# Gathering the attention matmuls of a tile step on TensorE ahead of 18 expert matmuls, from tile 16 on

## The chip, the cores and the metric

One core of one Trainium2 chip. The metric is the device time of one execution, in microseconds; lower is better.

## The reference, cut to what matters

Batched attention (8 batches, 8 heads, 512 local and 32 global tokens, head size 64) feeds an expert layer on its 8 x 544 output rows.

```python
s_g = scale * np.matmul(q_g, k_all.transpose(0, 1, 3, 2))       # global queries see all 544 keys
out_g = np.matmul(sm(s_g), v_all)
mask = np.abs(pos[:, None] - pos[None, :]) <= 32                # local queries: a band, and the 32 global keys
s_l = np.concatenate([s_lg, np.where(mask, s_ll, -1e9)], axis=-1)
out_l = np.matmul(sm(s_l), np.concatenate([v_g, v_l], axis=2))
h = np.maximum(np.maximum(x @ w1, x @ w2), x @ w3)              # x: 4608 rows of the attention's output, 512 wide; 768 wide inside
return h @ w_out
```

## The kernel before

A **tile** `sl` is 128 local queries of a pair `p` of heads; there are 128 tiles, four to a pair (`t = sl % 4`), sixteen to a batch `b`. The main loop (L506 to L535) makes one **step** per tile, and in a step TensorE serves several tiles at different stages, plus the expert layer of the batch before:

- **T**: `trans(sl + 1)` (L334), four 128x128 transposes of the next tile's probabilities, which a DMA put into `prob`. They go to the PSUM tile `T`, which ScalarE copies to `pt` (high part, L102) and from which VectorE subtracts (low part, L94).
- **S**: `scores(sl + 3)` (L300), four matmuls (two in the first tiles) into a PSUM tile `S`; VectorE reduces them (L322), ScalarE takes the exponential (L324), VectorE the reciprocal (L326, L327), GpSimd scales (L112), and a DMA stores to `prob` (L330).
- **O**: `pv(sl)` (L373), four value products of this tile with `pt` and `vs`, into `O`.
- **g**: `glob(p + 1, t)` (L262), in steps with `t` of 0 and 1 alone: two matmuls with the global queries of the next pair, of 384 columns at `t = 0` and 160 at `t = 1`, into a PSUM tile `S` as well. At `t = 2`, `glob_soft` (L285) finishes their softmax and stores it with six small DMAs to `probg`.
- **G**: `transg(sl + 1)` (L356), one 128x128 transpose of a third of `probg` into a PSUM tile `S`. ScalarE copies the wanted part to the last 32 columns of `pt` (L102), VectorE subtracts (L94).
- **L**: `fill(n)` (L470) takes `n` matmuls of the expert layer (L421: 216 per batch, then L440: 72), each 128x128 times 128x512. 18 per step make a batch's 288 in 16 steps.

Splitting into a high and a low part is how full fp32 accuracy is kept; the first 26 to 28 tiles skip it in part (`NATK`, `NAT`). From step 16 on the scores run three tiles ahead; before (`EARLY`) they run further ahead.

Tiles come from pools, and a pool with `bufs=n` hands out n buffers in turn: a new tile waits until every reader of the tile that last had its buffer is done. **`S` has two buffers (L61), shared by S, g and G**; `T` and `O` have one each, `pm` (the expert layer's sums) three. All eight PSUM banks are taken.

Every engine takes its instructions in a fixed order, which a scheduler sets when the kernel is built, mostly that of the code; where it reckons that an instruction isn't ready it lets later ones pass. `copy`, `sub` and `times` (L89 to L112) pick the engine by a running tally of each engine's load. All DMAs are issued by SyncE (SP) in one queue.

The kernel ends with the last batch's expert layer and that of the global rows (L537), without attention work beside them.

Of the kernel before, what the change touches and what calls it, by code (L numbers as in the profile page):

```python
# [47 lines left out]
def f32(ap):  # L48
    return ap.bitcast(F32)


def body(ctx, tc, kin, qin, vin, min_, w1, w2, w3, w4, out):
# [31 lines left out]
    def settle(ns):  # L84
        top = max(load.values()) - ns
        for e in load:
            load[e] = max(load[e], top)

    def sub(out, a, b, psum=False):  # L89
        n = width(out)  # L90
        c = {"d": n * 1.04 + (160 if psum else 110)}
        if not psum:
            c["p"] = n * 2.32 + 130
        (dve if least(c) == "d" else pool).tensor_tensor(out=out, in0=a, in1=b, op=ALU.subtract)  # L94

    def copy(out, a, psum=False):
        n = width(out)
        c = {"d": n * (1.04 if psum else 0.52) + (160 if psum else 150), "a": n * 0.833 + (150 if psum else 190)}
        if least(c) == "d":
            dve.tensor_copy(out=out, in_=a)  # L100
        else:
            act.copy(out=out, in_=a)  # L102
# [107 lines left out]
    EARLY, AHEAD = 16, 9  # L210
    kraw, kst, qraw, qs, vraw, vs, xr, sc, pg, pts = [{} for _ in range(10)]

    def load_k(p):
        if p < B * NP:
            if 4 * p in NATK:
                kraw[p] = att.tile([128, KW + 2 * SG], F32, name="kn", tag="kst")
            else:
                kraw[p] = att.tile([128, KW + 2 * SG], F32, name="kraw", bufs=1)
            nc.sync.dma_start(out=kraw[p], in_=kin[p])

    def split_k(p):
        if p >= B * NP or 4 * p in NATK:
            return
        r = kraw.pop(p)
        g = r[:, KW:].rearrange("p (j g) -> p j g", j=2)
        t = qgz
        copy(t[:, :, 0:SG], g)
        sub(t[:, :, 64:64 + SG], g, f32(t)[:, :, 0:SG])
        t = kst[p] = att.tile([128, 2, KW], F32R, name="kst")
        copy(t[0:64, 0], r[0:64, 0:KW])  # L230
        copy(t[64:128, 1], r[64:128, 0:KW])
        sub(t[64:128, 0], r[0:64, 0:KW], f32(t)[0:64, 0])
        sub(t[0:64, 1], r[64:128, 0:KW], f32(t)[64:128, 1])
# [21 lines left out]
    def split_v(s):  # L255
        if NAT <= s < NS:
            v = vraw.pop(s)
            t = vs[s] = att.tile([128, 4, 2, D], F32R, name="vs")
            copy(t[:, :, 0], v)
            sub(t[:, :, 1], v, f32(t)[:, :, 0])  # L260
# [24 lines left out]
    def glob_soft(p):  # L285
        if p >= B * NP:
            return
        s, nm, z = pg[p]
        dve.tensor_tensor(out=nm[:, 0:1], in0=nm[:, 0:1], in1=nm[:, 1:2], op=ALU.min)
        act.activation(out=s, in_=s, func=AF.Exp, bias=nm[:, 0:1], scale=-1.0, accum_out=z[:, 0:1])  # L290
        dve.tensor_scalar(out=z[:, 0:1], in0=z[:, 0:1], scalar1=1e-9, scalar2=None, op0=ALU.add)
        dve.reciprocal(out=z[:, 0:1], in_=z[:, 0:1])
        spend("d", 220)
        spend("a", 760)
        times(s, s, z[:, 0:1])

        for c0, n, i, h, d0 in GPUT:
            nc.sync.dma_start(out=f32(probg[p % 2])[64 * h:64 * h + 64, i, d0:d0 + n], in_=s[:, c0:c0 + n])
# [35 lines left out]
    def trans(sl):  # L334
        if sl >= NS:
            return
        s = sc.pop(sl)
        ps = psT.tile([128, 512], F32, name="T")
        pr = ps.bitcast(F32R)
        for j in range(2):  # L340
            for c in range(2):
                i = pe.transpose(pr[:, 256 * j + 128 * c:256 * j + 128 * c + 128], s[:, j, 128 * c:128 * c + 128], identr)  # L342
        if sl == EARLY:

            ctx.enter_context(tc.issue_after(i.ins))
        src = ps.rearrange("p (x q) -> p x q", q=128)
        if sl < NAT:
            pt = pts[sl] = att.tile([128, 2, 2, 160], F32, name="pt", tag="pt")
            copy(pt.rearrange("p j c q -> p (j c) q")[:, :, 0:128], src, True)
        else:  # L350
            pt = pts[sl] = att.tile([128, 2, 2, 2, 160], F32R, name="pt", tag="pt")
            v = pt.rearrange("p j c a q -> p (j c) a q")
            copy(v[:, :, 0, 0:128], src, True)
            sub(v[:, :, 1, 0:128], src, f32(v)[:, :, 0, 0:128], True)

    def transg(sl):  # L356
        if sl >= NS:
            return
        p, t = divmod(sl, 4)
        pt = pts[sl]  # L360
        i, h, n = GCH[t]
        g = psS.tile([128, 512], F32, name="S")
        pe.transpose(g.bitcast(F32R)[:, 0:128], probg[p % 2][:, i], identr)  # L363
        src = g[:, 64 * h:64 * h + 64 * n].rearrange("p (c j g) -> p c j g", j=2, g=SG)
        if sl < NAT:
            copy(pt.rearrange("p j c q -> p c j q")[:, 0:n, :, 128:160], src, True)
            return
        v = pt.rearrange("p j c a q -> p c j a q")
        hi, lo = v[:, 0:n, :, 0, 128:160], v[:, 0:n, :, 1, 128:160]
        copy(hi, src, True)  # L370
        sub(lo, src, f32(hi), True)
# [39 lines left out]
    def moe_group(xs, n, stores):  # L411
        hh = []
        for f in range(6):
            ht = moe.tile([128, 2, 512], F32R, name=f"h{f}", tag=f"h{f}")
            m = moe.tile([128, 512], F32, name="m", tag="m")
            for i in range(3):
                ps = pm.tile([128, 512], F32, name="pm")
                q = 0
                for k in range(4):
                    for w, a in ((wh, 0), (wh, 1), (wl, 0)):  # L420
                        pe.matmul(ps[:, 0:n], lhsT=w[f][:, i, k], rhs=xs[k][:, a, 0:n], start=(q == 0), stop=(q == 11))  # L421
                        q += 1
                        if q < 12:
                            yield
                if i == 0:
                    copy(m[:, 0:n], ps[:, 0:n], True)
                else:
                    spend("d", n * 1.04 + 67)
                    dve.tensor_tensor(out=m[:, 0:n], in0=ps[:, 0:n], in1=m[:, 0:n], op=ALU.max)  # L429
                if i == 2:  # L430
                    copy(ht[:, 0, 0:n], m[:, 0:n])
                    sub(ht[:, 1, 0:n], m[:, 0:n], f32(ht)[:, 0, 0:n])
                yield
            hh.append(ht)
        for t in range(n // 128):
            ps = pm.tile([128, 512], F32, name="pm")
            q = 0
            for f in range(6):
                for a, w in ((0, wo[0]), (1, wo[0]), (0, wo[1])):
                    pe.matmul(ps, lhsT=hh[f][:, a, 128 * t:128 * t + 128], rhs=w[:, f], start=(q == 0), stop=(q == 17))  # L440
                    q += 1
                    if q < 18:
                        yield
            o = moe.tile([128, 512], F32, name="o", tag="o", bufs=2)
            copy(o, ps, True)
            stores(t, o)
            yield
# [3 lines left out]
    def moe_local(b):  # L451
        def st(t, o):
            r = b * TOK + SG + t * 128
            nc.sync.dma_start(out=out[r:r + 128], in_=o)
        return moe_group(xs.pop(b), SL, st)
# [14 lines left out]
    def fill(n):  # L470
        if mm[0]:
            for _ in range(n):
                next(mm[0], None)
# [3 lines left out]
    def next_scores(last):  # L477
        while ahead[0] <= last:
            scores(ahead[0])
            split_q(ahead[0] + 1)  # L480
            load_q(ahead[0] + 4)
            ahead[0] += 1
# [23 lines left out]
    for sl in range(NS):  # L506
        p, t = divmod(sl, 4)
        b, n = divmod(p, NP)
        settle(4500)
        if sl % 16 == 0 and b:  # L510
            fill(400)
            mm[0] = moe_local(b - 1)
        trans(sl + 1)
        fill(4)
        next_scores(max(min(sl + 5, EARLY - 1), sl + 3))
        if t == 2:
            split_k(p + 2)
            load_k(p + 3)
        fill(4)
        pv(sl)  # L520
        if t <= 1:
            glob(p + 1, t)
        elif t == 2:
            glob_soft(p + 1)
        fill(3)
        transg(sl + 1)
        fill(7)
        split_v(sl + 2)
        load_v(sl + 3)
        for _ in range(WS[sl] if sl < len(WS) else 0):  # L530
            weight_step()
        if sl % 16 >= 12:
            i = sl % 16 - 12
            q = b * NP + i
            xs.setdefault(b, []).append(split_x(xr[q][:, :, 0:128], SL))  # L535
# [56 lines left out]
```

## Time and profile before

| | |
|---|---|
| time, median of 3 runs | 860.52 us (859.49 to 860.64) |
| span of the profiled execution | 861.4 us |
| busy: TensorE, VectorE, ScalarE, GpSimd | 94%, 66%, 61%, 59% of the span |
| mean granted TensorE clock | 0.973 of full speed |

The profiled execution's own time is its span, 861.4 us from the first to the last instruction; what lies around it is not in the view, and the span is 0.9 us above the median of the three runs. "PE" is TensorE's matmuls, "PEld" its weight loads, "DVE" VectorE, "ACT" ScalarE, "POOL" GpSimd, "SPq" SyncE's DMA issues. In rows of a timeline stand the start in us from the span's start, the duration, engine, line, operation, output<-inputs, shape and count, and in brackets the engine's idle time before it with what ended it. Matmuls overlap in such rows (a duration holds the way through the array), so TensorE's pace is read from start to start.

### The profile page before, as it was taken

The numbers are of one execution on the slowest core, as the hardware profiler recorded it, in microseconds if no ns is written. First come the engines' busy times: TensorE is split into PE (matmuls) and PEld (weight loads), VectorE is DVE, ScalarE is ACT, GpSimd is POOL, SyncE is SP. The second block draws the span as 40 slices with busy tenths as digits, with TensorE's granted clock in tenths as the row PEclk, the third lists the DMA queues.
The fourth block names the chain that finished last, engine by engine and source line by source line (L and its number), as shares of the span: only waits on it lengthen the run. The fifth ranks groups of instructions, "written<-read, shape, count | busy, mean of one in ns | idle before, by whom it ended". The sixth has DMA issues, their size and how long they took to land.

```text
span 861.4 us, 15721 instructions
## 1 busy us (share of the span) xinstructions
PE 813.0 (94%) x4452; PEld 674.2 (78%) x4452; DVE 566.7 (66%) x1784; ACT 529.1 (61%) x1479; POOL 509.8 (59%) x683
## 2 busy tenths in 40 slices
PE   5866788999999999999999999999999999999997
PEld 3644566778888788888888888888888888888896
DVE  4657699787777677777778677867787676511111
ACT  4656566677767676767776767776776766511111
POOL 4535577786667666776768576766677664411211
PEclk8786999999999999999999999999999999999999
DMA  6586655424333533344333533353334322100000
GB/s 201 166 243 186 190 165 190 146 90 153 103 106 96 160 112 106 100 123 125 104 109 100 150 98 100 96 160 111 112 111 131 121 75 72 62 24 1 25 25 25
DMA packets 107238, 98.53 MB, mean 114 GB/s; under 512 B 21008, under 2 KB 97936, under 8 KB 107152
## 3 DMA queue, kind: packets, MB, share of 16 engines
q1 hardware_dynamic: 107152, 97.53, 37.2%
q8 instruction: 36, 0.59, 0.3%
q14 instruction: 50, 0.41, 0.2%
HBM read 56.85 MB, written 8.91 MB: 76 GB/s over the span
## 4 chain that ended last, share of the span: by engine, by line
PE 82%; DVE 6%; DMA 6%; ACT 2%; issue 2%; SPq 2%; POOL 1%; ACTq 0%; POOLq 0%; DVEq 0%
PE pm L421 45%; PE pm L440 16%; PE O L390 6%; PE S L319 5%; PE T L342 4%; DMA wraw<-w_in 2%; PE S L277 1%; DVE wraw L170 1%; DMA probg<-sg 1%; PE O L383 1%; PE S L363 1%; PE pm L315 1%; DMA early<-s 1%; ACT s L324 1%; PE S L315 1%
## 5 line engine op out<-in xcount | busy, mean ns | idle before, releaser
L421 PE MATMUL pm<-xs,wh 128*128 128x512 f32 (+1 forms) x1296 | 408.0, 388 | 3.3 <-POOL xs L94 3.3
L421 PEld LDWEIGHTS pm<-xs,wh 128*128 128x128 f32 x1296 | 233.6, 189 | 35.3 <-POOL xs L94 3.8
L421 PE MATMUL pm<-xs,wl 128*128 128x512 f32 (+1 forms) x648 | 253.1, 391 | 0.0
L112 POOL TENSOR_SCALAR s<-s,z 128x192 f32<-128x192 f32 (+1 forms) x250 | 113.0, 465 | 98.7 <-ACT lox L102 37.8
L421 PEld LDWEIGHTS pm<-xs,wl 128*128 128x128 f32 x648 | 122.5, 189 | 22.7 <-issue 1.6
L324 ACT ACTIVATE s<-s,nm 128x192 f32<-128x192 f32 (+1 forms) x256 | 118.0, 462 | 26.6 <-DVE nm L322 22.6
L440 PE MATMUL pm<-woh,h 128*128 128x512 f32 x408 | 133.7, 398 | 0.1
L94 POOL TENSOR_TENSOR h<-m,h 128x512 fp32r<-128x512 f32 (+1 forms) x54 | 69.3, 1283 | 95.4 <-ACT h L102 93.9
L429 DVE TENSOR_TENSOR m<-pm,m 128x512 f32<-128x512 f32 (+1 forms) x108 | 71.1, 659 | 72.2 <-PE pm L421 72.0
L94 POOL TENSOR_TENSOR qs<-qraw,qs 128x256 fp32r<-128x256 f32 x100 | 73.8, 749 | 56.3 <-ACT qs L102 45.3
L94 DVE TENSOR_TENSOR pt<-T,pt 128x512 fp32r<-128x512 f32 x102 | 70.5, 691 | 46.4 <-ACT pt L102 44.5
L322 DVE CUSTOM_DVE_ANT_0 s<-S,mask 128x192 f32<-128x192 f32 (+1 forms) x232 | 77.9, 371 | 18.5 <-PE S L315 7.7
L326 DVE TENSOR_SCALAR z<-z 128x2 f32<-128x2 f32 x128 | 52.0, 406 | 49.8 <-ACT s L324 49.2
L440 PEld LDWEIGHTS pm<-woh,h 128*128 128x128 f32 x408 | 74.7, 188 | 12.1 <-POOL h L94 0.5
L440 PE MATMUL pm<-wol,h 128*128 128x512 f32 x204 | 81.8, 401 | 0.0
L94 POOL TENSOR_TENSOR vs<-vraw,vs 128x256 fp32r<-128x256 f32 x102 | 75.8, 744 | 8.2 <-ACT vs L102 4.0
L94 POOL TENSOR_TENSOR kst<-kraw,kst 64x576 fp32r<-64x576 f32 x49 | 70.4, 1436 | 11.8 <-issue 8.2
L102 ACT CAST pt<-T 128x512 fp32r<-128x512 f32 x90 | 52.7, 586 | 36.0 <-PE T L342 36.0
L102 ACT CAST qs<-qraw 128x256 fp32r<-128x256 f32 x100 | 40.5, 407 | 54.8 <-PE S L319 54.3
L390 PEld LDWEIGHTS O<-pt,vs 128*128 128x128 f32 x408 | 66.4, 188 | 9.1
L390 PE MATMUL O<-pt,vs 128*128 128x320 f32 (+1 forms) x408 | 72.8, 300 | 0.0
L342 PEld LDWEIGHTS T<-identr,prob 128*128 128x128 f32 x448 | 50.5, 141 | 25.1 <-DMA prob<-s 2.6
(95 smaller groups left out, 1292.2 us busy)
## 6 DMA issues: line engine op xcount, KB each, us to landing
vraw<-v_in SPq DMA_DIRECT2D x128, 128.0 KB, 2.4
qraw<-q_in SPq DMA_DIRECT2D x100, 128.0 KB, 2.2
prob<-s SPq DMA_DIRECT2D x56, 224.0 KB, 2.4
prob<-s SPq DMA_DIRECT2D x56, 192.0 KB, 2.3
wraw<-w_in SPq DMA_DIRECT2D x18, 512.0 KB, 5.3
out_dram<-o SPq DMA_DIRECT2D x32, 256.0 KB, 2.6
kraw<-k_in SPq DMA_DIRECT2D x25, 320.0 KB, 3.1
qn<-q_in SPq DMA_DIRECT2D x28, 128.0 KB, 3.4
```

What stands on the lines that cost most here:

```text
L94: (dve if least(c) == "d" else pool).tensor_tensor(out=out, in0=a, in1=b, op=ALU.subtract)
L102: act.copy(out=out, in_=a)
L112: pool.tensor_scalar(out=out, in0=a, scalar1=col, scalar2=1.0, op0=ALU.mult, op1=ALU.mult)
L319: pe.matmul(ph[j][:, 0:n], lhsT=qs[sl][:, a, 128 * j:128 * j + 128], rhs=kst[p][:, j, c0:c0 + n], start=(a == 0), stop=(a == 1))
L322: dve.tensor_tensor_reduce(out=s[:, j, 0:n], in0=ph[j][:, 0:n], in1=mask[:, (1, 0, 1, 0)[t], 32 * (t == 0):32 * (t == 0) + n], scale=-0.12 ...
L324: act.activation(out=s[:, j, 0:n], in_=s[:, j, 0:n], func=AF.Exp, bias=nm[:, j:j + 1], scale=-1.0, accum_out=z[:, j:j + 1])
L326: dve.tensor_scalar(out=z, in0=z, scalar1=1e-9, scalar2=None, op0=ALU.add)
L342: i = pe.transpose(pr[:, 256 * j + 128 * c:256 * j + 128 * c + 128], s[:, j, 128 * c:128 * c + 128], identr)
L390: pe.matmul(o[:, j, 0:320].rearrange("p (a q) -> p a q", a=2)[:, :, 0:n], lhsT=vs[sl][:, 2 * j + c].rearrange("p a d -> p (a d)"), rhs=pt[ ...
L421: pe.matmul(ps[:, 0:n], lhsT=w[f][:, i, k], rhs=xs[k][:, a, 0:n], start=(q == 0), stop=(q == 11))
L429: dve.tensor_tensor(out=m[:, 0:n], in0=ps[:, 0:n], in1=m[:, 0:n], op=ALU.max)
L440: pe.matmul(ps, lhsT=hh[f][:, a, 128 * t:128 * t + 128], rhs=w[:, f], start=(q == 0), stop=(q == 17))
```

## The change

From step 16 on (`EARLY`), the transpose G moves from behind the value products up to right behind T, and the 18 expert matmuls, until now in four portions (4 behind T, 4 behind S, 3 behind O and g, 7 behind G), stand in one portion behind everything else. Which instructions are issued does not change, apart from a few copies, subtractions and scalings that the tally gives to another engine.

```diff
+        steady = sl >= EARLY
         trans(sl + 1)
-        fill(4)
+        if steady:
+            transg(sl + 1)
+        else:
+            fill(4)
         next_scores(max(min(sl + 5, EARLY - 1), sl + 3))
...
-        fill(4)
+        if not steady:
+            fill(4)
         pv(sl)
         if t <= 1:
             glob(p + 1, t)
         elif t == 2:
             glob_soft(p + 1)
-        fill(3)
-        transg(sl + 1)
-        fill(7)
+        if steady:
+            fill(18)
+        else:
+            fill(3)
+            transg(sl + 1)
+            fill(7)
```

TensorE in step 68 (`t = 0`, pair 17), from the scores S to the transpose G, before; the PSUM tiles `S` are numbered in the order in which they are made.

```order
L319 MATMUL S_5212<-kst_4742,qs_5153 128x192 x4
L421 MATMUL pm_5207<-xs_4702,wh2_104 128x512
L421 MATMUL pm_5207<-xs_4702,wl2_110 128x512
L421 MATMUL pm_5207<-xs_4796,wh2_104 128x512 x2
L390 MATMUL O_5238<-pt_5129,vs_5119 128x320
L390 MATMUL O_5238<-pt_5129,vs_5119 128x2x128
L390 MATMUL O_5238<-pt_5129,vs_5119 128x320
L390 MATMUL O_5238<-pt_5129,vs_5119 128x2x128
L277 MATMUL S_5252<-kst_5071,qgz_96 128x384 x2
L421 MATMUL pm_5207<-xs_4796,wl2_110 128x512
L421 MATMUL pm_5207<-xs_4871,wh2_104 128x512 x2
L363 MATMUL S_5260<-identr_87,probg1_95 128x128
```

The same step after, from the transposes T to the first expert matmuls:

```order
L342 MATMUL T_5197<-identr_87,prob1_93 128x128 x4
L363 MATMUL S_5205<-identr_87,probg1_95 128x128
L319 MATMUL S_5209<-kst_4741,qs_5153 128x192 x4
L390 MATMUL O_5231<-pt_5129,vs_5119 128x320
L390 MATMUL O_5231<-pt_5129,vs_5119 128x2x128
L390 MATMUL O_5231<-pt_5129,vs_5119 128x320
L390 MATMUL O_5231<-pt_5129,vs_5119 128x2x128
L277 MATMUL S_5245<-kst_5068,qgz_96 128x384 x2
L421 MATMUL pm_5252<-xs_4623,wh2_104 128x512 x2
```

The order in which the step's three `S` tiles are made was S, g, G and is G, S, g. With two buffers, g used to take over the buffer of G of the step before, and now takes over that of G of its own step, with four S and four O between the two and no L; the wait that is built into g's first matmul is for VectorE's reading of that G.

VectorE around T, S and G of this step, before:

```order
L94 TENSOR_TENSOR pt_5202<-T_5197,pt_5202 128x4x128
L322 ISA s_5213,nm_5214<-S_5212,mask_89 128x192
L322 ISA nm_5214 128x1
L322 ISA s_5213,nm_5214<-S_5212,mask_89 128x192
L322 ISA nm_5214 128x1
L326 TENSOR_SCALAR z_5215<-z_5215 128x2
L327 RECIPROCAL z_5215<-z_5215 128x2
L396 TENSOR_TENSOR lox_5244<-O_5238,lox_5244 64x320
L398 TENSOR_TENSOR xr_5239<-O_5238,lox_5244 64x160 x2
L281 ISA sg_5249,nmg_5250<-S_5252,sg_5249 64x384
L281 ISA nmg_5250 64x1
L94 TENSOR_TENSOR pt_5202<-S_5260,pt_5202 128x2x2x32
```

and after:

```order
L94 TENSOR_TENSOR pt_5202<-T_5197,pt_5202 128x4x128
L94 TENSOR_TENSOR pt_5202<-S_5205,pt_5202 128x2x2x32
L322 ISA s_5210,nm_5211<-S_5209,mask_89 128x192
L322 ISA nm_5211 128x1
L322 ISA s_5210,nm_5211<-S_5209,mask_89 128x192
```

The low part of G (`pt<-S`) moved from the end of the step's VectorE work to right behind the low part of T (`pt<-T`), ahead of the reductions of S.

ScalarE, after, in the same step:

```order
L102 CAST pt_5202<-T_5197 128x4x128
L102 CAST h1_5096<-m_5097 128x512
L102 CAST pt_5202<-S_5205 128x2x2x32
L102 CAST kst_5391<-kraw_5073 64x576
L324 ACTIVATE s_5210,z_5212<-s_5210,nm_5211 128x192 x2
L102 COPY lox_5237<-O_5231 64x320
```

The high part of G moved in the same way: it stands behind that of T, in this step with an expert copy (`h`) between them, and ahead of the exponentials; at `t = 1` it stands directly behind that of T.

## The prediction

> **What bounds the kernel now.** I read the page's head first, then the windows by stage, then TensorE's timeline inside one step, and last VectorE's and ScalarE's timelines beside it.
>
> ```profile
> span 861.4 us, 15721 instructions
> PE 813.0 (94%) x4452; PEld 674.2 (78%) x4452; DVE 566.7 (66%) x1784; ACT 529.1 (61%) x1479; POOL 509.8 (59%) x683
> ```
>
> ```profile
> 88.70:191.00 102.30, 89.94 (x477) 68.30 (x478) 81.52 (x209) 66.03 (x177) 72.23 (x77) 0.97 0.50 155
> 191.00:400.00 209.00, 207.89 (x1151) 176.11 (x1151) 154.93 (x505) 149.36 (x421) 143.71 (x201) 1.00 0.40 120
> 400.00:742.00 342.00, 342.00 (x1892) 289.80 (x1891) 256.11 (x834) 241.83 (x683) 233.67 (x326) 1.00 0.36 109
> ```
>
> The columns of the windows are the stretch, its length, the busy time of PE, PEld, DVE, ACT and POOL, the granted clock, the DMA share and GB/s. The changed steps run from about 88.7 us (step 16) to 742 us and fall into two stages. From 191 us on PE is busy for 549.9 of 551 us at full clock: what is put into TensorE's row or taken out of it counts in full, and the other engines have 25 to 30% to spare. Before 191 us weights are still being converted, and PE idles 12.4 of 102.3 us.
>
> PE's pace is read from start to start. Step 68, and at the end O of step 69:
>
> ```profile
> 412.63 0.46 PE L342 MATMUL T<-identr,prob 128*128 128x128 f32 x4
> 412.93 0.70 PE L421 MATMUL pm<-xs,wh 128*128 128x512 f32 x2
> 413.46 0.40 PE L421 MATMUL pm<-xs,wl 128*128 128x512 f32 x1
> ...
> 413.93 0.59 PE L319 MATMUL S<-kst,qs 128*128 128x192 f32 x4
> 414.35 0.41 PE L421 MATMUL pm<-xs,wh 128*128 128x512 f32 x1
> ...
> 415.29 0.69 PE L390 MATMUL O<-pt,vs 128*128 128x320 f32 x4
> 415.82 0.51 PE L277 MATMUL S<-kst,qgz 128*128 128x384 f32 x2
> 416.16 0.40 PE L421 MATMUL pm<-xs,wl 128*128 128x512 f32 x1
> ...
> 416.86 0.22 PE L363 MATMUL S<-identr,probg 128*128 128x128 f32 x1
> 416.91 0.45 PE L421 MATMUL pm<-xs,wl 128*128 128x512 f32 x1
> 417.20 0.63 PE L421 MATMUL pm<-xs,wh 128*128 128x512 f32 x2
> 417.67 0.39 PE L421 MATMUL pm<-xs,wl 128*128 128x512 f32 x1
> ...
> 418.59 0.45 PE L342 MATMUL T<-identr,prob 128*128 128x128 f32 x4
> ...
> 421.26 0.74 PE L390 MATMUL O<-pt,vs 128*128 128x320 f32 x4
> 421.83 0.35 PE L277 MATMUL S<-kst,qgz 128*128 128x160 f32 x2
> ```
>
> Two undisturbed L take 417.67 - 417.20 = 0.47, so one takes 0.235 us. The four T take 0.30 to the next start, and the two L behind them 0.53 where 0.47 is usual: a tail of 0.06. G takes 0.05, and the L behind it 0.29, a tail of 0.055. The four S take 0.42, the four O 0.53 (0.57 in step 69), the two g 0.34 (0.19). There is no gap in the row: L, T, S, O, g and G all stand ready when PE comes to them. The whole step takes 418.59 - 412.63 = 5.96 us.
>
> **The change part by part.**
>
> *What is gained on PE.* The number of matmuls stays. A tail comes where a short matmul is followed by one that must load other weights. T's tail before an L goes; G's stays, since S loads weights of the same size behind it. So a step gains between nothing (T's tail falls on G) and 0.06 us; I take 0.03, as G loads as T does. Over the 98 steps of a full PE row (27 to 124) that is -2.9 us (0 to -5.9). The Trainium skill, "TensorE: Matmul & The Clock Gate", section "LDWEIGHTS (loading the stationary operand)", prices a weight load by its 128 columns alone, 128 / 1.2 GHz = 107 ns, whatever the matmul behind it. The four S, of 192 columns, bear it out at 0.42 / 4 = 0.105 us each, and the four T at 0.30 / 4 = 0.075 do not; by the rule this term would be nothing.
>
> *What is added: g waits for G of its own step.* After the change g takes over the buffer of a G that stands only four S and four O ahead. In PE's row g's turn comes, counted from the start of T, at 0.30 + 0.03 (T) + 0.11 (G with its tail) + 0.42 (S) + 0.53 (O) = 1.39 us at t = 0 and 1.43 at t = 1. But it may start only when VectorE has read G, and the low part of G stands behind the low part of T on VectorE, which needs ScalarE's copy of T. These rows price that chain (ScalarE, then VectorE):
>
> ```profile
> 413.18 0.59 ACT L102 CAST pt<-T 128x512 fp32r<-128x512 f32 x1 [1.39 <-PE T L342]
> 413.67 0.62 ACT L102 CAST h<-m 128x512 fp32r<-128x512 f32 x1
> ...
> 417.96 0.27 ACT L102 CAST pt<-S 128x128 fp32r<-128x128 f32 x1
> ...
> 423.12 0.21 ACT L102 CAST pt<-S 128x64 fp32r<-128x64 f32 x1
> ```
>
> ```profile
> 413.80 0.69 DVE L94 TENSOR_TENSOR pt<-T,pt 128x512 fp32r<-128x512 f32 x1 [0.17 <-ACT pt L102]
> ...
> 418.98 0.28 DVE L94 TENSOR_TENSOR pt<-S,pt 128x128 fp32r<-128x128 f32 x1
> ...
> 423.91 0.23 DVE L94 TENSOR_TENSOR pt<-S,pt 128x64 fp32r<-128x64 f32 x1
> ```
>
> From the start of T (412.63), ScalarE's copy runs from 0.55 to 1.14 and VectorE's subtraction from 1.17 to 1.86; neither waits for more than its input. At t = 0 ScalarE then does `h` (1.04 to 1.66) and the high part of G (1.56 to 1.83), and VectorE the low part from 1.86 to 2.14. At t = 1 there is no `h`: the low part follows at once, 1.79 to 2.02. What a release of PE costs is seen where S waited for ScalarE's reading of a buffer:
>
> ```profile
> 145.16 0.24 ACT L102 COPY pt<-S 128x128 f32<-128x128 f32 x1
> ```
>
> ```profile
> 145.46 1.02 PE L315 MATMUL S<-kn,qn 128*128 128x224 f32 x4 [0.93 <-ACT pt L102]
> ```
>
> 145.46 - 145.40 = 0.06. With that and 0.06 for a weight load that now nothing hides (the tail above), g starts at 2.26 instead of 1.39 at t = 0, 0.87 late, and at 2.14 instead of 1.43 at t = 1, 0.71 late. Behind g on PE stand the step's 18 L, which have everything they need and can't pass it. So a pair loses 1.58 us, and the pairs 8 to 31 (their g runs in steps 28 to 121) are 24: 37.9 us, and 0.7 for step 25, 38.6 in all. Bounds: without the tail, the 0.03 and the `h`, 1.2 a pair, 29 us; with ScalarE or VectorE one operation of 0.6 behind in every other step, 2.2 a pair, 53 us. Nothing else on PE can cover it.
>
> *What the moved copies hold up.* The two `pt<-S` now stand ahead of the exponentials and reductions of S, which costs these at most 0.27 + 0.28 us; but S itself stands four L earlier (0.94 us). The product is needed two steps later. Nothing is lost; without those four L it would be up to 0.5 us a step. Eighteen L in a row finish one or two sums of twelve, of which `pm` holds three, so that VectorE has 24 x 0.235 = 5.6 us to clear one, and PE isn't held there.
>
> *G comes earlier than its data may.* At t = 3, G reads the next pair's `probg`, of which the first and the fourth of six DMAs are needed:
>
> ```profile
> 426.52 3.70 SPq L298 DMA_DIRECT2D probg<-sg  x6
> ```
>
> ```profile
> probg<-sg SPq DMA_DIRECT2D x64, 16.0 KB, 1.8
> ```
>
> ```profile
> 430.07 0.46 PE L342 MATMUL T<-identr,prob 128*128 128x128 f32 x4
> ...
> 434.02 0.22 PE L363 MATMUL S<-identr,probg 128*128 128x128 f32 x1
> ```
>
> The fourth issues at 426.52 + 3 x 0.62 = 428.38 and lands 1.8 later, at 430.2. Now that G comes at 434.02; changed, it would come 0.33 behind T, at 430.40. The chain that leads to these DMAs begins with the g of t = 1, so it lies later by 0.7 at most, as T does, and by up to 0.5 more where it queues behind the moved copies; in the last pair of a batch an output store (L454) also stands between the six on SP, which takes about as long to issue as one of them. It is a tie: 0 to 0.5 us for 24 pairs, 0 to 12; I take 0.1, +2.4, near the landing above.
>
> *The first stage.* Here PE's longest wait is for such a DMA:
>
> ```profile
> 152.40 0.25 PE L363 MATMUL S<-identr,probg 128*128 128x128 f32 x1 [2.71 <-DMA probg<-sg]
> ```
>
> ```profile
> PE T L342 <- DMA prob<-s: 6.5, 5, 2.1
> ```
>
> G now comes 11 L and O earlier, 11 x 0.235 + 0.5 = 3.1 us, for three pairs: up to +9, and some +3 for their g. Against that S stands 0.94 earlier in each step, which can shorten the five waits of T for its DMA by that much each, to -5. I take +3 (-5 to +12), since the quoted wait shows that such a G is awaited.
>
> *Sum.* 861.4 - 2.9 + 38.6 + 2.4 + 3 = 902.5; the median of the runs lies 0.9 below the span, so **901 us**.
>
> **The rivals.** (1) *The wait is covered, and the kernel is faster.* If g's buffer were read within 1.4 us of the start of T, only the lost tails and shorter waits of T would be left: 860.5 - 2.9 - 2 = 856. For it: all the work around is unchanged, and now PE waits for nothing. Against it: T's two readings alone end at 1.86. It decides if VectorE takes G before T, or if g gets another buffer. Chance 0.06.
>
> (2) *The copies or `probg` become the bound.* If ScalarE and VectorE, whose work now comes in one burst behind each cluster, run late into the next T, or G at t = 3 waits its full 0.5, the upper bounds 53, 12 and 12 come together: 33 us above my terms, 934; half of that is 918. DVE's 256.11 of 342.00 us speaks against a lasting queue. Chance 0.08.
>
> (3) *The clock falls.* After the 2.71 us wait above PE was slow:
>
> ```profile
> 153.32 0.63 PE L421 MATMUL pm<-xs,wl 128*128 128x512 f32 x1
> 153.75 0.67 PE L342 MATMUL T<-identr,prob 128*128 128x128 f32 x4
> ```
>
> An L took 0.43 instead of 0.235. If each of the 48 waits of g were followed by some eight such L, 48 x 8 x 0.195 = 75 us would come on top, 976. Against it: after a wait of 1.11 us the clock of its window, 191 to 400 us, stayed at 1.00:
>
> ```profile
> 297.00 0.51 PE L342 MATMUL T<-identr,prob 128*128 128x128 f32 x4 [1.11 <-DMA prob<-s]
> ```
>
> The Trainium skill, same page, section "A second HAM failure mode: psum-queue depth-cycling", says that short idles of PE that recur with every round of a PSUM buffer can throw the clock to half and back, as these would. One wait of 1.11 does not show what 48 do. Chance 0.04.
>
> (4) *No change.* The scheduler keeps the old order, or tails and waits cancel. Its order shows the cluster in every step from 27 on. Chance 0.02.
>
> **How the numbers follow.** My forecast has 0.80. Its own range is 861.4 - 0.9 with 29 to 53 for g and part of the other bounds, 884 to 918; the rivals outside hold 0.2, so this is also the range for 8 in 10. A measurement here tells 0.2%, 1.7 us, from no change. Faster: rival 1, 0.06. Same: 0.02. Slower: 0.92.
>
> **What would show it.** Right: from 191 us on, PE's timeline has an idle of 0.6 to 0.9 us before each g, released by VectorE's `pt` of L94, none in steps with t = 2; step 68 takes about 6.8 us instead of 5.96, and a step without g some 0.03 less than now; VectorE's and ScalarE's busy times stay. Wrong: g follows O within 0.1 us, or PE waits at T or S instead, or the clock falls below 1.00 after 191 us.

## The result and the profile after

| | before | after |
|---|---|---|
| median time, us | 860.0 (857.97 to 860.64, 4 runs) | 903.11 (898.92 to 907.56, 4 runs) |
| span of the profiled execution, us | 861.4 | 902.6 |

The change makes the kernel slower: the ratio of the times is 1.051, with an interval of 1.047 to 1.055. The runs also spread wider, 8.6 us where it was 2.7.

The head of the page of after, to be set against that of before:

```profile
span 902.6 us, 15688 instructions
...
PE 823.6 (91%) x4452; PEld 683.2 (76%) x4452; DVE 542.9 (60%) x1782; ACT 521.0 (58%) x1478; POOL 508.7 (56%) x686
```

No engine got new work: VectorE (by 24 us), ScalarE and GpSimd are busy less than before, and TensorE, with the same 4452 matmuls, is busy 10.6 us more. So the 41.2 us are idle time of PE and matmuls that run slower, and the windows say where. I cut both traces at the T of tile 17 and the T of tile 28, the two ends of the first stage, and at the T of tile 126. First before, then after (columns as in the prediction):

```profile
88.70:173.20 84.50, 72.72 (x384) 54.33 (x385) 65.80 (x162) 52.36 (x138) 56.86 (x59) 0.96 0.56 172
173.20:742.00 568.80, 567.11 (x3135) 479.87 (x3134) 426.76 (x1384) 404.86 (x1144) 392.75 (x544) 1.00 0.37 112
```

```profile
85.00:177.50 92.50, 77.17 (x385) 58.86 (x386) 66.80 (x169) 52.77 (x141) 56.73 (x59) 0.89 0.52 158
177.50:783.50 606.00, 575.86 (x3136) 485.65 (x3135) 402.37 (x1379) 395.84 (x1137) 391.02 (x545) 0.99 0.34 105
```

The first stage costs 8.0 us more and the long second one 37.2. What lies ahead of the first changed step is 3.7 us shorter in this execution, which is no work of the change: the last two experiments below, whose instructions stand in the order of before up to there, took 85.4 us as well, so it was before's profiled execution that started late. The tail behind tile 126 is 0.3 us shorter. In the second stage PE's idle time is read as length less busy time: 568.80 - 567.11 = 1.7 us before, 606.00 - 575.86 = 30.1 us now. PE's waits in that window of after name who it waited for (total us, times, longest):

```profile
PE S L277 <- DVE pt L94: 28.8, 46, 2.6
PE S L363 <- DMA probg<-sg: 1.3, 3, 0.7
```

It is the wait that the prediction had named: g, L277, for VectorE's low part of G, in 46 of the 48 steps that have a g (in steps 48 and 112 g hardly waited: 0.07 us and nothing). One such step, PE's timeline from T to T:

```profile
433.43 0.46 PE L342 MATMUL T<-identr,prob 128*128 128x128 f32 x4
433.72 0.25 PE L363 MATMUL S<-identr,probg 128*128 128x128 f32 x1
433.81 0.66 PE L319 MATMUL S<-kst,qs 128*128 128x192 f32 x4
434.30 0.71 PE L390 MATMUL O<-pt,vs 128*128 128x320 f32 x4
435.63 0.62 PE L277 MATMUL S<-kst,qgz 128*128 128x384 f32 x2 [0.62 <-DVE pt L94]
436.08 0.63 PE L421 MATMUL pm<-xs,wh 128*128 128x512 f32 x2
...
440.22 0.29 PE L342 MATMUL T<-identr,prob 128*128 128x128 f32 x2
```

The same stretch on ScalarE and then on VectorE:

```profile
433.98 0.59 ACT L102 CAST pt<-T 128x512 fp32r<-128x512 f32 x1 [2.05 <-PE S L363]
434.46 0.62 ACT L102 CAST h<-m 128x512 fp32r<-128x512 f32 x1
434.98 0.27 ACT L102 CAST pt<-S 128x128 fp32r<-128x128 f32 x1
```

```profile
434.60 0.69 DVE L94 TENSOR_TENSOR pt<-T,pt 128x512 fp32r<-128x512 f32 x1 [0.28 <-ACT pt L102]
435.28 0.29 DVE L94 TENSOR_TENSOR pt<-S,pt 128x128 fp32r<-128x128 f32 x1
```

The chain is there link by link: T's copy on ScalarE ends at 434.57, `h` follows, G's high part at 434.98, T's low part on VectorE from 434.60 to 435.29, G's low part to 435.57, and g starts 0.06 us later, at 435.63. The bracket shows 0.62 us of idle, less than what the wait costs, since a matmul's row holds its way through the array. From start to start: O began at 434.30 and takes 0.53, so g's turn came at 434.83 and g is 0.80 late. Its two matmuls then take 435.63 to 436.08, 0.45 us where they took 0.34: their first weight load starts with g, at 435.63, where it started 0.12 us ahead of g before (415.70 and 415.82).

### The profile page after: what moved, and what is told of

The parts are those of the page before. It is cut to its first block, busy times and chain, and to the rows that moved or that the text cites. A ratio compares the mean times of both kernels' runs of the same rounds, so it can differ in the third digit from the quotient of the medians.

```text
span 902.6 us, 15688 instructions
## 1 busy us (share of the span) xinstructions
PE 823.6 (91%) x4452; PEld 683.2 (76%) x4452; DVE 542.9 (60%) x1782; ACT 521.0 (58%) x1478; POOL 508.7 (56%) x686
## 4 chain that ended last, share of the span: by engine, by line
PE 71%; DVE 10%; ACT 6%; DMA 5%; issue 3%; POOL 2%; SPq 2%; ACTq 0%; POOLq 0%; DVEq 0%
PE pm L421 40%; PE pm L440 15%; DVE pt L94 4%; ACT pt L102 3%; PE T L342 3%; PE O L390 3%; PE S L277 3%; PE S L319 3%; DMA probg<-sg 2%; PE S L363 1%; PE S L315 1%; DVE wraw L170 1%; PE O L383 1%; PE S L273 1%; DMA wraw<-wo_in 1%
## 5 line engine op out<-in xcount | busy, mean ns | idle before, releaser
L421 PE MATMUL pm<-xs,wh 128*128 128x512 f32 (+1 forms) x1296 | 388.7, 383 | 3.6 <-POOL xs L94 3.6
L421 PEld LDWEIGHTS pm<-xs,wh 128*128 128x128 f32 x1296 | 236.2, 190 | 47.4 <-POOL xs L94 4.1
L421 PE MATMUL pm<-xs,wl 128*128 128x512 f32 (+1 forms) x648 | 247.7, 382 | 0.0
L112 POOL TENSOR_SCALAR s<-s,z 128x224 f32<-128x224 f32 (+1 forms) x253 | 112.5, 458 | 131.3 <-ACT lox L102 75.0
L440 PE MATMUL pm<-woh,h 128*128 128x512 f32 x408 | 128.5, 396 | 0.0
L326 DVE TENSOR_SCALAR z<-z 128x2 f32<-128x2 f32 x128 | 42.1, 329 | 67.3 <-ACT s L324 66.5
L390 PE MATMUL O<-pt,vs 128*128 128x320 f32 (+1 forms) x408 | 74.9, 305 | 0.0
L319 PE MATMUL S<-kst,qs 128*128 128x192 f32 (+1 forms) x400 | 66.5, 288 | 0.0
L398 DVE TENSOR_TENSOR xr<-O,lox 64x160 f32<-64x160 f32 x204 | 64.3, 315 | 2.7
```

What stands on the lines that cost most here:

```text
L112: pool.tensor_scalar(out=out, in0=a, scalar1=col, scalar2=1.0, op0=ALU.mult, op1=ALU.mult)
L319: pe.matmul(ph[j][:, 0:n], lhsT=qs[sl][:, a, 128 * j:128 * j + 128], rhs=kst[p][:, j, c0:c0 + n], start=(a == 0), stop=(a == 1))
L390: pe.matmul(o[:, j, 0:320].rearrange("p (a q) -> p a q", a=2)[:, :, 0:n], lhsT=vs[sl][:, 2 * j + c].rearrange("p a d -> p (a d)"), rhs=pt[ ...
L398: dve.tensor_tensor(out=xr[p][64 * j:64 * j + 64, t], in0=o[0:64, j, 0:160], in1=lo[:, j], op=ALU.add)
```

## The experiments

Two theories stood. The **buffer theory**: with two buffers for S, g and G, each g takes over the buffer that G of its own step has just filled, and PE waits until VectorE has read it. The **burst theory**: the copies and reductions that now fall due together behind each cluster cost the time, wherever g stands. "First stage" and "second stage" below are the windows between the same three T as above (84.5 and 568.8 us before, 92.5 and 606.0 after). Diffs are against the changed kernel, and ratios against the kernel before.

### g moved away from G

```diff
         pv(sl)
+        if steady:
+            fill(6)
         if t <= 1:
             glob(p + 1, t)
...
         if steady:
-            fill(18)
+            fill(12)
```

> The changed kernel, but g and the start of the global softmax stand behind 6 of the 18 L instead of ahead of all 18. Buffer theory (g waits because, of two S buffers, it takes over that of G of its own step, whose reading ends about 2.2 us after the start of T): g's turn now comes at 1.4 + 6 x 0.23 = 2.8 us, so the waits at g are gone, the gain of about 0.06 us a step stays, and what the first stage (steps 16 to 26) lost stays too: 861 us, 855 to 866. Burst theory (what costs is that all copies of a step fall due at once, with no L between, and PE then waits here or there): the waits only move elsewhere, 890 to 905.

Measured: 877.1 us, ratio 1.0226 (1.0208 to 1.0244); stages 92.0 and 577.9. It recovers most of the loss in the second stage, but not all. PE's waits in the second stage (195 to 740 us, as for all the kernels below):

```profile
PE S L319 <- DVE nmg L281: 3.2, 9, 0.6
PE S L363 <- DMA probg<-sg: 3.0, 5, 1.2
...
PE S L277 <- DVE pt L94: 0.2, 1, 0.2
```

The wait for `pt` fell to 0.2 us, from 25.2 in after between the same times, as the buffer theory says, but its 861 was missed: the late g is now read too late for a later S (L319 waits for `nmg`), G at t = 3 waits for its DMA, and the first stage stayed as slow as after. Whether fewer than six L would do was not tried.

### G ahead of T

```diff
         steady = sl >= EARLY
-        trans(sl + 1)
         if steady:
             transg(sl + 1)
-        else:
+        trans(sl + 1)
+        if not steady:
             fill(4)
```

(With it, `pt` is allocated by whichever of the two comes first.)

> The changed kernel, but G stands ahead of T instead of behind it, on TensorE and so on ScalarE and VectorE; g stays right behind O with no L between, and the 18 L stay together. Buffer theory: G's copies no longer queue behind those of T; its low part ends about 0.9 us after the start of the cluster, before g's turn at 1.4, so the waits at g are gone: 861 us, 855 to 866; T's own copies come 0.3 us later, which nothing waits for until the next step. Burst theory: the same copies in the same burst, 890 to 905.

Measured: 885.07 us, ratio 1.0318 (1.0298 to 1.0339); stages 91.9 and 585.9. The waits of the second stage:

```profile
PE S L370 <- DMA probg<-sg: 7.7, 8, 1.8
PE S L277 <- DVE pt L94: 3.4, 5, 0.9
PE S L370 <- DVE xr L405: 3.1, 10, 0.4
```

(L370 is G here.) g's wait fell from 25.2 to 3.4 us although the copies still come in one burst, which speaks for the buffer theory; but its 861 failed again: G, which is earliest of all here, now waits itself, for its `probg` DMA and for VectorE.

### G behind g

```diff
         trans(sl + 1)
-        if steady:
-            transg(sl + 1)
-        else:
+        if not steady:
             fill(4)
...
         if steady:
+            transg(sl + 1)
             fill(18)
```

> Only the second half of the change: the 18 L stand together behind the cluster, but G stays behind g, in the order T, S, O, g, G. Buffer theory: g takes over the buffer of G of the step before and doesn't wait, but G takes over that of S of its own step at t = 0 and 1, whose reductions end behind T's low part at about 1.86 + 2 x 0.35 = 2.6 us, while G's turn is at about 1.6: G waits some 1.0 to 1.1 us in 48 steps, and none at t = 2 and 3; 51 us less the gain and plus the first stage: 910, 900 to 920. Burst theory: g and G stand later in the burst, so 890 to 905 with waits in steps of every t.

Measured: 900.95 us, ratio 1.0503 (1.0486 to 1.052); stages 87.7 and 606.6. The waits of the second stage hold one row:

```profile
PE S L363 <- DVE nm L322: 30.3, 44, 1.2
```

Now G waits instead, for the reading of S of its own step. The median step is 6.77 and 6.73 us long at t = 0 and 1, where there is a g, and 5.60 and 5.62 at t = 2 and 3. T, S, O and G are copied and reduced in one burst at all four. The wait follows the count of S tiles in a cluster: with three (S, G, g), the third waits for the first. The time itself lies in the ranges of both theories (900 to 920 and 890 to 905) and tells nothing; the steps do, as waits at t = 0 and 1 alone were what the buffer theory said.

### G moved alone, the large products left in their places

```diff
         if steady:
             transg(sl + 1)
-        else:
-            fill(4)
+        fill(4)
...
-        if not steady:
-            fill(4)
+        fill(4)
         pv(sl)
...
         if steady:
-            fill(18)
+            fill(10)
```

> Only the first half of the change: G right behind T, but the L stay spread out: 4 behind G, 4 behind S, 10 behind O and g. Buffer theory: g still takes over the buffer of G of its own step, but 8 L of 0.23 us stand between, so its turn is at 3.3 us, after the reading at 2.2: no waits at g, 860 us, and up to 868 if it is G's earlier place that costs in the first stage (it reads DMAs that land late there). Burst theory: the copies are spread as before, 860 too; this run tells what G's early place alone costs.

Measured: 875.29 us, ratio 1.0206 (1.0176 to 1.0236); stages 88.3 and 581.5. The waits of the second stage:

```profile
PE S L363 <- DMA probg<-sg: 11.2, 12, 1.9
```

g doesn't wait any more, with eight L between G and g. What is left there is one wait alone, the prediction's "tie": the G of t = 3 comes before its DMA. That fits that g's waits, now gone, had delayed it. The expectation missed this: it held up to 8 us for the first stage and nothing for this wait, which was 1.3 us in after.

### A third buffer, no instruction moved

```diff
-    pm = ctx.enter_context(tc.tile_pool(name="pm", bufs=3, space=PSUM))
-    psS = ctx.enter_context(tc.tile_pool(name="psS", bufs=2, space=PSUM))
+    pm = ctx.enter_context(tc.tile_pool(name="pm", bufs=2, space=PSUM))
+    psS = ctx.enter_context(tc.tile_pool(name="psS", bufs=3, space=PSUM))
```

> The changed kernel with its order of code untouched, but S gets three buffers and pm two instead of two and three. Buffer theory: g takes over a buffer that was read a step earlier, so its waits of 0.9 and 0.65 us are gone without moving an instruction; then T of t = 3 no longer comes 1.5 us later, and G at t = 3 waits for the probg DMAs as it did with G ahead of T and with G moved alone: 877, 868 to 887, unless pm with two buffers holds up the L, which would show as waits of L for VectorE. Burst theory: 895 to 905 as with two buffers.

Measured: 864.75 us, ratio 1.0072 (1.0049 to 1.0094); stages 87.0 and 571.8. The code's order is that of the change. PE's timeline at a step with t = 0, and then the waits of the second stage:

```profile
414.48 0.71 PE L390 MATMUL O<-pt,vs 128*128 128x320 f32 x4
415.03 0.51 PE L277 MATMUL S<-kst,qgz 128*128 128x384 f32 x2
```

```profile
PE S L363 <- DMA probg<-sg: 4.4, 5, 1.1
PE S L363 <- ACT pt L102: 0.9, 1, 0.9
```

g follows O at once, and 38 of the 43 us are gone. This settles it: the burst is whole, the cluster is whole, and without the buffer's hand-over the time is nearly that of before. The burst theory falls. That `pm` lost a buffer shows in no wait of L here. The expected 877 (868 to 887) was missed all the same: G's waits for `probg` came to 4.4 us, not to the 11.2 of G moved alone. The Trainium skill, "Perfetto Trace Analysis", section "Optimization Strategy", says that a gap which repeats on the engine that should be saturated can mean too few PSUM buffers for the next tile; the 46 gaps of g and this run agree.

### G moved alone, except at t = 3

As "G moved alone", but at t = 3 G stays between the last 3 and 7 L, where it was before the change: `if steady and t < 3: transg(sl + 1)`, and the old branch otherwise.

> G moved alone, L spread out, as in the run of that name, but at t = 3 G keeps its old place behind O and 11 L. If the 17 us that G's early place cost there are waits for the probg DMAs at t = 3, and nothing else: 859, 855 to 864, of which some 3 us are the first stage's. If G's early copies cost something at every t: 870 or more.

Measured: 858.11 us, ratio 0.9992 (0.9977 to 1.0007), no change that can be told; stages 86.2 and 565.0. Between 195 and 740 us PE waits nowhere. Against "G moved alone" this takes back 17 us by a change in one step out of four, 16.5 of them in the second stage, where that run's waits for `probg` add up to 12.8 us over the whole stage. So G's early place at t = 3 is shown as the cost, and the DMA wait as most of it.

### The cluster without its waits, from step 27 on

```diff
-        steady = sl >= EARLY
-        trans(sl + 1)
-        if steady:
+        steady = sl >= 27
+        if steady and t < 3:
             transg(sl + 1)
-        else:
+        trans(sl + 1)
+        if not steady:
             fill(4)
...
-        if steady:
+        if steady and t < 3:
             fill(18)
+        elif steady:
+            fill(11)
+            transg(sl + 1)
+            fill(7)
```

> The cluster without either wait: G ahead of T at t = 0 to 2, at t = 3 G behind O and 11 L as in the kernel before, 18 L together at t = 0 to 2, and all that from step 27 on, so that the first stage is the kernel before's. Buffer theory with probg as the second wait: only the gain is left, 0.06 us x 98 steps = 6 us: 852, 849 to 857. Burst theory: 870 or more.

Measured: 856.01 us, ratio 0.9956 (0.9938 to 0.9974); stages 85.6 and 565.5. (The helper for `pt` is that of "G ahead of T".) This is 0.4% faster than the kernel before, inside its expectation (849 to 857), but 4 us above the middle of it. In three steps of four all the attention matmuls stand together and 18 L behind them, and g's waits come to 1.5 us in all: gathering itself does no harm.

### T, S, O and g, then 9 L, G and 9 L, from step 27 on

```diff
-        steady = sl >= EARLY
+        steady = sl >= 27
         trans(sl + 1)
-        if steady:
-            transg(sl + 1)
-        else:
+        if not steady:
             fill(4)
...
         if steady:
-            fill(18)
+            fill(9)
+            transg(sl + 1)
+            fill(9)
```

> The other way round both waits: T, S, O, g in one cluster, then 9 L, G, 9 L, from step 27 on. g takes over the buffer of G of the step before; G takes over that of S of its own step, read at about 2.6 us, but stands at 3.7, and behind the probg DMAs at t = 3. Buffer theory: no waits, 852, 849 to 857; the gain is T's and S's tails. Burst theory: 870 or more.

Measured: 860.87 us, ratio 1.0021 (1.0007 to 1.0035); second stage 568.6. The expected 8 us didn't come, though PE hardly waits (0.4 us in all). The timeline says why:

```profile
408.11 0.66 PE L319 MATMUL S<-kst,qs 128*128 128x192 f32 x4
408.60 0.71 PE L390 MATMUL O<-pt,vs 128*128 128x320 f32 x4
409.16 0.51 PE L277 MATMUL S<-kst,qgz 128*128 128x384 f32 x2
409.50 0.40 PE L421 MATMUL pm<-xs,wh 128*128 128x512 f32 x1
```

Four S with O behind them take 408.60 - 408.11 = 0.49 us, where the prediction's row had 0.42 with an L behind; four O take 0.56 instead of 0.53. The tail that T lost turns up behind S: over the second stage, the median of the four S is 0.51 us ahead of O here and 0.435 ahead of an L in before. The cluster without its waits pays that too (0.51). What it saves besides is the tail behind G, which stays here, as the L behind G takes 0.28 us where a plain one takes 0.23.

### The change from step 27 on

```diff
-        steady = sl >= EARLY
+        steady = sl >= 27
```

> The changed kernel with the new order from step 27 on instead of 16. What the first stage costs is taken back, the waits at g stay. The profiled run of the changed kernel took 92.5 us from the T of step 16 to that of step 27 where the kernel before took 84.5: if these 8 us are the new order's, 895, 890 to 899; if they are chance, 901 to 905.

Measured: 891.55 us, ratio 1.0383 (1.0353 to 1.0413), 11.6 us below the change. Its windows, cut at the same three T:

```profile
85.40:169.20 83.80, 72.69 (x384) 54.31 (x385) 65.31 (x162) 52.51 (x137) 56.59 (x59) 0.96 0.56 174
169.20:770.50 601.30, 572.75 (x3135) 483.60 (x3134) 400.29 (x1383) 396.56 (x1143) 392.33 (x546) 1.00 0.34 106
```

The first stage is that of before again. So the first eleven changed steps cost 8.0 us in after's profile and some 11.6 us by the medians, where the prediction had 3.

### G moved, except at t = 3, from step 27 on

As "G moved alone, except at t = 3", with `steady = sl >= 27`.

> G moved alone at t = 0 to 2, L spread out, and that from step 27 on. In the steady steps the profile of the run without the last condition was 5.4 us below the kernel before (539.1 against 544.5 us over 94 steps), and its first stage 1.7 us above. With the first stage of the kernel before: 853.5, 851 to 856, and the same as the cluster without waits if it is T's tail alone that is gained; above 857 if the 5.4 us are chance.

Measured: 854.75 us, ratio 0.9951 (0.9931 to 0.9971): 0.5% faster than the kernel before, and not to be told from the cluster without its waits (0.9956). Its windows, cut at the same three T:

```profile
85.40:169.00 83.60, 72.79 (x385) 54.46 (x384) 65.46 (x161) 51.66 (x136) 56.08 (x59) 0.96 0.55 173
169.00:733.70 564.70, 562.86 (x3135) 481.13 (x3134) 417.06 (x1384) 402.09 (x1145) 391.37 (x545) 1.00 0.37 113
```

PE's busy time in the second stage is 4.2 us less than before with the same 3135 matmuls, and idle is 1.8 us against 1.7. What is gained here is tails: T and G side by side leave one tail in the L behind them where they used to leave two.

## Why the prediction was right

It said 901 us (884 to 918), slower, by g's wait for G; measured are 903.11 us and that wait. Point by point:

- **g's wait: right in mechanism and place, and near in size.** At t = 0 g starts 435.63 - 433.43 = 2.20 us after T (predicted 2.26), and its turn came at 1.40 (1.39). Late by 0.80, and 0.11 for the load: 0.91 us against 0.87. At t = 1:

```profile
440.22 0.46 PE L342 MATMUL T<-identr,prob 128*128 128x128 f32 x4
...
441.10 0.77 PE L390 MATMUL O<-pt,vs 128*128 128x320 f32 x4
442.21 0.46 PE L277 MATMUL S<-kst,qgz 128*128 128x160 f32 x2 [0.35 <-DVE pt L94]
442.50 0.66 PE L421 MATMUL pm<-xs,wh 128*128 128x512 f32 x2
```

  1.99 after T (2.14), its turn at 441.10 + 0.57 = 441.67 or 1.45 (1.43); late by 0.54, its two matmuls 0.29 instead of 0.19, so 0.64 against 0.71. The idle in the brackets, which the prediction had named as its sign at 0.6 to 0.9 us, is smaller: mostly 0.61 to 0.67 at t = 0 and 0.35 to 0.55 at t = 1. A pair loses 1.55 us where 1.58 was forecast. Three buffers without any other order (864.75) and as many copies in one burst (856.01) show that the buffer is the cause.
- **The steps.** Medians over tiles 32 to 126, before and after: t = 0 5.96 and 6.79 us (predicted about 6.8 for step 68), t = 1 5.89 and 6.46, t = 2 5.59 and 5.56, t = 3 5.68 and 5.59. No g, no wait, as predicted. VectorE's busy time did not stay, as the prediction had it: it fell by 24 us, and no run here shows why.
- **The gain: mis-sized, and made up of other tails.** The steps without g lost 0.03 and 0.09, on average 0.06, not 0.03: the upper bound of that term, -5.9 instead of -2.9. The means of the 23 steps with t = 2 between 32 and 123 show its parts. The 18 L take 4.12 us instead of 4.28, as no L stands behind T or G any more (those took 0.30 and 0.28 where a plain L takes 0.23). Against that the four S take 0.07 more ahead of O than ahead of an L, G takes 0.02 more behind T, and O 0.015 more. So G's tail went as well, which the prediction had left in place, and S got one that it had not foreseen; that the balance came out at its bound is luck. The rule that it had quoted from the Trainium skill, "TensorE: Matmul & The Clock Gate", section "LDWEIGHTS (loading the stationary operand)", a load by its columns alone, by which the term would be nothing, does not fit these figures.
- **`probg` at t = 3: right, but smaller while g waits.** 1.3 us instead of 2.4. Once g doesn't wait it is the next limit, 4.4 us with three buffers and 11.2 with G moved alone, which fits that each wait of g gives the DMA more time.
- **The first stage: the failed term.** +3 was forecast, inside bounds of -5 and +12; +8.0 in the profile. PE's waits there (85 to 177.5 us):

```profile
PE S L363 <- DMA probg<-sg: 4.9, 1, 4.9
PE S L363 <- ACT pt L102: 3.9, 1, 3.9
PE pm L421 <- POOL xs L94: 3.6, 1, 3.6
PE S L277 <- DVE pt L94: 1.6, 1, 1.6
PE T L342 <- DMA prob<-s: 1.3, 2, 1.0
```

  As forecast, G waits longer for `probg` (4.9, and 4.0 before) and T less for `prob` (1.3, and 2.8 before). The bound of -5 was read wrong: its five waits of T are a row over the whole execution, and this stage had two. Not forecast was G's wait of 3.9 for ScalarE's `pt`, at 122.42 us. ScalarE's timeline shows how it arose:

```profile
119.50 0.62 ACT L102 CAST h<-m 128x512 fp32r<-128x512 f32 x1
121.63 0.62 ACT L178 CAST wh<-cut 128x512 fp32r<-128x512 f32 x1 [1.51 <-DVE cut L171]
122.16 0.21 ACT L102 COPY pt<-S 128x64 f32<-128x64 f32 x1
```

  The G two `S` tiles earlier, at 117.50, had its copy behind that of a weight (`wh`), which itself waited 1.51 us for VectorE; the next G takes over its buffer, and starts when that copy is done. Idle grew by 15.3 - 11.8 = 3.5 us; the other 4.5 us are PE's busy time, 77.17 instead of 72.72, at a granted clock of 0.89 instead of 0.96. The term left out the clock.
- **Rival 3, the clock: partly true.** It had a chance of 0.04 as a fall behind each g. In the second stage it happened behind two long waits, here at 681.65 us:

```profile
681.65 0.61 PE L277 MATMUL S<-kst,qgz 128*128 128x384 f32 x2 [1.63 <-DVE pt L94]
682.11 1.01 PE L440 MATMUL pm<-woh,h 128*128 128x512 f32 x2
...
685.48 0.43 PE L440 MATMUL pm<-wol,h 128*128 128x512 f32 x1
```

  The eight L up to 685.75 take 3.64 us instead of 8 x 0.23 = 1.85: 1.8 us lost, at a granted clock of 0.59; behind the 2.56 us wait at 187.74 six took 2.36 us, 1.0 lost. A clock below 1.00 after 191 us was a sign of being wrong for the prediction: taken over all of 191 to 783.5 us it stayed at 1.00, and the two stretches cost 2.8 us of the 37.2.

The second stage can be closed from these: a pair's four steps are 0.83 + 0.57 - 0.03 - 0.09 = 1.28 us longer, 24 pairs 30.7; three g waits of 1.60, 1.63 and 2.56 us of idle instead of 0.62 add 3.9, the slow clock adds 2.8, and the two g that hardly waited take off about 1.5: 35.9 of 37.2 us, and the rest is not assigned. The waits of 1.60 and 1.63 stand where the tally had given VectorE a copy for the expert layer, so that T's and G's low parts queued behind it; at the one of 2.56, VectorE was at two operations for `xs` from 183.29 to 186.19 us. VectorE at the wait of 1.63, in step 108:

```profile
678.66 1.19 DVE L100 CAST xs<-xr 128x512 fp32r<-128x512 f32 x1
679.77 0.68 DVE L429 TENSOR_TENSOR m<-pm,m 128x512 f32<-128x512 f32 x1
680.38 0.68 DVE L94 TENSOR_TENSOR pt<-T,pt 128x512 fp32r<-128x512 f32 x1
681.30 0.29 DVE L94 TENSOR_TENSOR pt<-S,pt 128x128 fp32r<-128x128 f32 x1 [0.25 <-ACT pt L102]
```

By the spans, 902.5 us was forecast and 902.6 measured (902.5 - 0.9 is 901.6, which the prediction gives as 901). That it came so close is partly luck, as misses cancel. In the second stage the forecast was too high by the gain, by `probg` and by the two g without a wait (3, 1 and 1.5 us), and too low by the long waits and the clock (6.7 us that no term had); over the whole, it was 5 us too low for the first stage (8 to 9 by the medians), and after's execution reached step 16 earlier than before's by 3.7 us. Open stays how much of the first stage each of its waits and the clock cost; no run separates them.

## What to carry to other kernels

Before moving a matmul, write down the turn order of every pool that its output shares with others: three tiles of a two-buffer pool in one cluster make the third wait for the first's readers, and that costs more (1.55 us a pair) than all tails that gathering saves (about 0.24). A reader that is moved forward must also be set against the landing of its data, and where two waits lie on one path, removing the first shows the second: four of the expectations above missed for that reason or for a tail that only moved, and a fifth, that of the third buffer, took the second wait for larger than it was. What was worth having of this change is about 4 us: G beside T where its data is early enough, with or without the rest of the cluster, and only where the engine is already full.

## What the runs showed of the hardware

- The granted clock fell to about half after some waits of PE and stayed after others of the same length. In after it fell behind waits of 1.61 (at 165.88, granted 0.60 from there to 170.00), 1.63 and 2.56 us, and not behind one of 1.60 (at 288.27, granted 1.00 to 292.00). In the change from step 27 on, waits of 1.62 (at 277.75) and 1.61 (at 670.01) left it at 1.00. With G moved alone, one of 1.91 (at 295.84) left it at 1.00 and another of 1.91 (at 484.69) brought it to 0.61; with G ahead of T, one of 1.16 (at 163.83) brought it to 0.59. So no length of wait between 1.2 and 1.9 us decides it here. The slow stretch, once there, ended some 3 to 4 us after the wait. The Trainium skill, "TensorE: Matmul & The Clock Gate", section "HAM oscillation — how this bites in real kernels", gives idle gaps of over about 3.4 us as what to avoid; here less than half of that was enough at times. Its section "What's actually happening" says that the clock's window runs free of the kernel, which would fit that equal waits differ; no run here shows the window.
- A matmul's cost depends on what stands beside it: four S take 0.42 to 0.44 us ahead of an L and 0.49 to 0.51 ahead of O. T and G each leave a tail in an L behind them (it takes 0.30 and 0.28 us instead of 0.23); side by side they leave one (0.30, and G takes 0.09 instead of 0.06), and with no L behind either they leave none there. Such tails are most of the 3 to 4 us by which the second stage of T, S, O, g, 9 L, G, 9 L (568.6 us) is longer than those of the other three orders that hardly wait (564.7 to 565.5).
